# Attention and two gated layers on one core: a pair's softmax sums inverted as a row and spread over the partitions by way of DRAM

## Chip, core and metric

The kernel runs on one core of one Trainium2 chip. The metric is the device time of one execution in microseconds (us), as the median of several executions. Engines are named as in the profile: PE (matmul), PEld (PE's weight load, which overlaps the matmuls), DVE (vector engine), ACT (scalar engine), POOL (GpSimd), SP (the engine that issues all DMAs here).

## The reference, cut to what matters

Two batches, 8 heads, 1152 keys, head size 64; queries are averaged in pairs, so there are 576 queries per head. The output of attention is the input of a layer with a rational gate (512 to 2048 to 512), and that of a second layer with a SiLU gate (512 to 1536 to 512). The change is in attention's last line but one:

```python
q_pool = q.reshape(B, H, S // 2, 2, D).mean(axis=3)          # 576 queries
scores = scale * np.matmul(q_pool, k.transpose(0, 1, 3, 2))
scores = scores - np.max(scores, axis=-1, keepdims=True)
attn = np.exp(scores)
attn = attn / (np.sum(attn, axis=-1, keepdims=True) + 1e-09)
return np.matmul(attn, v).astype(np.float32)
```

The kernel multiplies the unnormalized exponentials with the values and divides by the sums afterwards.

## The kernel before, in words

**Stages.** Attention fills the first 290 us; the first layer follows, then a norm and the second layer. All matmuls are float32; the layers' weights come as 64-bit numbers and are converted in the kernel (lines 171 to 232), in part while attention runs. The converted pairs of that part are stored to DRAM (line 237, "spill") and fetched later.

**Attention.** The 16 heads are worked on in 8 pairs. A pair has 9 tiles of 128 queries (`TILES`): four of head 0, one shared by both heads (64 queries each), four of head 1. For a tile, PE makes the scores (L755), DVE takes their maximum (L784), ACT the exponentials and their sum into one column of `sums` [128 x 9] (L790), PE transposes the exponentials (L805), and DVE or ACT copy them out of PSUM into `pt` (L837, L840). The next tiles' scores go into the PSUM banks that these copies free.

**After the tiles of a head** (`pair_ops`, L867): 18 steps per head multiply the values with `pt` (L908; head size on the partitions, 576 queries in two halves of 288 columns, on partitions 0 to 63 and 64 to 127 of the one `av` bank). Two copies per head take the halves out of PSUM into `xt` [128 x 576], where head 0 has partitions 0 to 63 and head 1 the others (lines 589 and 592, which serve other copies too). The inverse sums have a query on each partition, while `xt` has a query in each column; so once per pair `f_rinv` adds 1e-9 and inverts [128 x 9] on DVE (L882, L883), `f_rx` spreads each inverse over 64 columns on POOL (L891, L893), `f_rows` transposes four blocks of 128 x 128 into the `prep` bank (L955) and `f_rT` a fifth into the `av` bank (L941), which ACT copies to `rxh` (L945). DVE then multiplies `xt`'s first 512 columns by the bank (`f_div`, L959), and POOL or DVE the last 64 by `rxh`, in two parts (`f_div_rest`, L964). Lines 592 and 605 split `xt` into the high and low parts `x_hi`, `x_lo` that the first layer reads. The bank `prep` has one buffer and serves the transposes of keys and queries as well (L703).

**What sets the order.** Operations are written down as `Op(engine, cost, key, function, needs, buffers)`, and `order()` places them in a planned time: on each engine the one of lowest key among those that can start now. An `op_any` may go to one of several engines. PE's tile and value steps are chained by a list written out by hand (`seq` in `attention`): scores of two tiles, up to five value steps, the transposes of both tiles. Each engine runs its operations in the planned order; a DMA counts 2000 ns in the plan from its issue to whoever needs it. All of attention and the first parts of the first layer (`FINE`) are placed in a first plan, the rest in a second, behind it on each engine.

Of the kernel before, what the change touches and what calls it, by code (L numbers as in the profile page):

```python
# [8 lines left out]
F32 = mybir.dt.float32  # L9
F32R = mybir.dt.float32r  # L10
U32 = mybir.dt.uint32
AF = mybir.ActivationFunctionType
ALU = mybir.AluOpType
AX = mybir.AxisListType
PSUM = bass.MemoryType.PSUM
# [4 lines left out]
def attention_moe_moe2_kernel(  # L20
# [18 lines left out]
    nc = tc.nc  # L39
    B, H, S, D = q.shape  # L40
    SQ = S // 2
# [8 lines left out]
    HALF = SQ % 128  # L50
    NFULL = SQ // 128
# [7 lines left out]
    def pool(tag, bufs=1, space=None):  # L59
        if tag not in pools:  # L60
            kw = {} if space is None else {"space": space}
            pools[tag] = scope[-1].enter_context(tc.tile_pool(name=tag, bufs=bufs, **kw))
# [3 lines left out]
    def T(tag, shape, dtype=F32, space=None):  # L66
        pool(tag, BUFS.get(tag, 1), space)
        return pools[tag].tile(shape, dtype, tag=tag, name=tag)
# [7 lines left out]
    ident = T("ident", [128, 128])  # L76
# [340 lines left out]
    PE, DVE, ACT, POOL = "PE", "DVE", "ACT", "POOL"  # L417

    def cost(eng, n):
        return {PE: 0.425 * n, DVE: 70 + 1.04 * n, ACT: 60 + 0.834 * n, POOL: 148 + 2.104 * n}[eng]  # L420
# [132 lines left out]
    NQ = NFULL + 1  # L553
# [4 lines left out]
    for h in range(2):  # L558
# [3 lines left out]
    NP = len(heads) // 2  # L562
    ABUF = {
        "kn": 2, "vn": 3, "qn0": 1, "qn1": 1, "qp": 2, "kT0": 1, "kT1": 1, "qT0": 1, "qT1": 1,
        "prep": 1, "av": 1, "p": 2, "pt": 3, "nm": 3, "sums": 2, "xt": 2, "rinv": 1, "rx": 1, "rxh": 1,
        "spill": 2,
    }
    BUFS.update(ABUF)
# [10 lines left out]
    NT = len(TILES)  # L579

    QW = SQ // 2
    TS = 3100

    def copy_ways(dst, src, n, psum=False, scale=None, fast=False, seen=lambda ins: None):

        by = 1.0 if scale is None else scale

        def on_act():
            seen(nc.scalar.activation(dst(), src(), AF.Copy, scale=by))

        def on(eng):
            seen(eng.tensor_scalar(dst(), src(), by, 1.0, op0=ALU.mult, op1=ALU.mult))

        ways = [(ACT, cost(ACT, n), on_act), (DVE, 70 + (0.52 if fast else 1.04) * n, lambda: on(nc.vector))]
        if not psum:
            ways.append((POOL, 30 + 1.08 * n, lambda: on(nc.gpsimd)))
        return ways

    def op_any(ways, key, deps=(), bufs=()):
        eng, c, fn = ways[0]  # L600
        return Op(eng, c, key, fn, deps, bufs, ways[1:])

    def sub_ways(out, a, b, n):
        def on(eng):
            eng.tensor_sub(out(), a(), b().bitcast(F32))

        return [(POOL, cost(POOL, n), lambda: on(nc.gpsimd)), (DVE, cost(DVE, n), lambda: on(nc.vector))]
# [125 lines left out]
    pt, pt_buf, pt_op, sums, sum_buf, sum_op, xt_ops, xt_buf, x_op = ({} for _ in range(9))  # L733
# [130 lines left out]
    LAST = [NFULL, 2 * NFULL]  # L864
    AVG = [[kt] for kt in range(NKT)]

    def pair_ops(pr):  # L867

        e = {}
        xb = Buf("xt")  # L870
        rb, rxb, rhb = Buf("rinv"), Buf("rx"), Buf("rxh")
        base = NT * pr * TS
        added = []

        def x_():
            if "x" not in e:
                e["x"] = T("xt", [128, SQ])
            return e["x"]

        def f_rinv():  # L880
            e["rinv"] = T("rinv", [128, NT])
            nc.vector.tensor_scalar_add(e["rinv"], sums[pr], 1e-9)  # L882
            nc.vector.reciprocal(e["rinv"], e["rinv"])  # L883

        def f_rx():
            rx = e["rx"] = T("rx", [128, NFULL + 1, 2, 64])
            rinv = e["rinv"]
            for h in range(2):
                r0 = h * (NFULL + 1)
                src = rinv[:, r0:r0 + NFULL].unsqueeze(2).to_broadcast([128, NFULL, 64])  # L890
                nc.gpsimd.tensor_scalar(rx[:, 0:NFULL, h, :], src, 1.0, 1.0, op0=ALU.mult, op1=ALU.mult)  # L891
            src = rinv[:, NFULL:NFULL + 1].unsqueeze(2).to_broadcast([128, 2, 64])
            nc.gpsimd.tensor_scalar(rx[:, NFULL], src, 1.0, 1.0, op0=ALU.mult, op1=ALU.mult)  # L893

        kr = base + NT * TS + 0
        o_rinv = Op(DVE, 330, kr, f_rinv, sum_op[pr], [sum_buf[pr], rb])
        o_rx = Op(POOL, 1050, kr + 300, f_rx, [o_rinv], [rb, rxb])

        for h in range(2):
            ab = Buf("av")  # L900
            last = None
            key = base + LAST[h] * TS + 9500

            def f_av(kt, h=h):
                if kt == 0:
                    e["av", h] = T("av", [128, 512], F32, space=PSUM)
                for c in range(2):
                    nc.tensor.matmul(  # L908
                        e["av", h][64 * c:64 * c + 64, 0:QW],
                        lhsT=v_tile[2 * pr + h][:, KEYS[kt], :],  # L910
                        rhs=pt[pr, h][:, kt, c * QW:(c + 1) * QW],
                        start=(kt == 0),
                        stop=(kt == NKT - 1),
                    )

            def f_avs(g, f=f_av):
                for kt in AVG[g]:
                    f(kt)

            for g in range(len(AVG)):  # L920
                last = Op(
                    PE, len(AVG[g]) * 0.84 * 2 * QW, key + 1350 * g, lambda g=g, f=f_avs: f(g),
                    [last, v_op[2 * pr + h], *pt_op[pr, h]], [ab, v_buf[2 * pr + h], pt_buf[pr, h]],
                )
                last.mode = "columns"
                av_ops.append((LAST[h] + NT * pr, last))
            key += 4000
            m = slice(64 * h, 64 * h + 64)
            for c in range(2):

                def src_(c=c, h=h):
                    return e["av", h][64 * c:64 * c + 64, 0:QW]

                def to_(c=c, m=m):
                    return x_()[m, c * QW:(c + 1) * QW]

                added.append(op_any(copy_ways(to_, src_, QW, True), key + 100 * c, [last], [ab, xb]))
            if h == 1:

                def f_rT():  # L940
                    nc.tensor.transpose(e["av", 1][:, 384:512], e["rx"][:, NFULL].rearrange("p a d -> p (a d)"), ident)  # L941

                def f_rxh():
                    e["rxh"] = T("rxh", [128, 128])
                    nc.scalar.activation(e["rxh"], e["av", 1][:, 384:512], AF.Copy)  # L945

                o_rT = Op(PE, 120, key - 200, f_rT, [o_rx, last], [ab, rxb])
                o_rxh = Op(ACT, 170, key - 100, f_rxh, [o_rT], [ab, rhb])

        pb = Buf("prep")  # L950

        def f_rows():
            e["rb"] = T("prep", [128, 512], F32, space=PSUM)
            for t in range(NFULL):
                nc.tensor.transpose(e["rb"][:, t * 128:t * 128 + 128], e["rx"][:, t].rearrange("p a d -> p (a d)"), ident)  # L955

        def f_div():
            x = e["x"]
            nc.vector.tensor_mul(x[:, 0:512], x[:, 0:512], e["rb"])  # L959

        def f_div_rest(eng):
            x = e["x"]
            for s in (slice(0, 64), slice(64, 128)):
                eng.tensor_mul(x[s, 512:SQ], x[s, 512:SQ], e["rxh"][s, s])  # L964

        o_rows = Op(PE, 460, key - 200, f_rows, [o_rx], [pb, rxb])
        o_div = [
            Op(DVE, 600, key + 800, f_div, [*added, o_rows], [pb, xb]),
            op_any(
                [(POOL, 566, lambda: f_div_rest(nc.gpsimd)), (DVE, 280, lambda: f_div_rest(nc.vector))],  # L970
                key + 800, [*added, o_rxh], [xb, rhb],
            ),
        ]
        b, hp = divmod(pr, H // 2)

        def xs(l):
            return (x_hi, x_lo)[l][:, hp, b * SQ:(b + 1) * SQ]

        o_xh = op_any(copy_ways(lambda: xs(0), x_, SQ, fast=True), key + 2000, o_div, [xb])
        x_op[b, hp] = op_any(sub_ways(lambda: xs(1), x_, lambda: xs(0), SQ), key + 2500, [o_xh], [xb])  # L980

    def f_warm():
# [513 lines left out]
```

## Time and profile before

| what | value |
|---|---|
| median of 3 executions | 745.83 us (742.72 to 746.51) |
| the profiled execution | 745.6 us |
| its span, first to last instruction | 743.8 us |
| PE, DVE, ACT, POOL busy, share of the span | 94%, 75%, 54%, 38% |
| mean granted clock of PE, share of the full 2.4 GHz | 0.986 |

The profile is of one execution. A busy share is an average over stages with different limits, and PE's matmuls are pipelined, so that two of them overlap in the records: the time from start to start of neighbours is what a matmul takes of the stream. The chain of waits follows the end back to what released each step; its shares say which engine's time went straight into the span.

### The profile page before, as it was taken

Reading aid. Unit: us, or ns where it says so; the run is one execution under the profiler, and the core shown is the slowest. Engines: PE = TensorE matmul, PEld = TensorE weight load, DVE = VectorE, ACT = ScalarE, POOL = GpSimd, SP = SyncE. Lnnn points to the kernel's source line nnn. Section 1 sums busy time; section 2 is a strip of 40 time slices with the busy share of each in tenths; the row PEclk is TensorE's granted clock in tenths of the full one; section 3 lists DMA queues with packets and bytes.
Section 4 is the critical chain, followed back from the end, with each engine's and each line's share of the span. In section 5 each row is a group of like instructions: output and inputs, shape, how many; then the busy total and the mean of one; then the engine's idle time right before and its main releaser. Section 6 shows DMA issues by size and latency. Waiting matters only on the chain.

```text
span 743.8 us, 13108 instructions
## 1 busy us (share of the span) xinstructions
PE 699.0 (94%) x5257; PEld 604.0 (81%) x5257; DVE 556.3 (75%) x723; ACT 403.4 (54%) x633; POOL 280.6 (38%) x245
## 2 busy tenths in 40 slices
PE   8899989998998999899999899899999999999997
PEld 7666666666666668889889799798999899989996
DVE  4799998988878773987977859957769346854844
ACT  4767677677777764898745756416423222312210
POOL 3032455645455520444442352326436123612500
PEclk9999989999999999999999999999999999999999
DMA  7444465446445330223104104000224202420103
GB/s 207 117 155 129 122 214 179 161 162 234 162 150 184 129 115 28 87 85 114 58 16 155 56 1 142 29 28 1 62 82 142 85 29 85 135 93 29 57 1 127
DMA packets 51596, 77.13 MB, mean 104 GB/s; under 512 B 4176, under 2 KB 33872, under 8 KB 51536
## 3 DMA queue, kind: packets, MB, share of 16 engines
q1 hardware_dynamic: 51536, 76.30, 31.6%
q8 instruction: 41, 0.67, 0.4%
q14 instruction: 19, 0.16, 0.1%
HBM read 61.87 MB, written 14.42 MB: 103 GB/s over the span
## 4 chain that ended last, share of the span: by engine, by line
PE 62%; DVE 20%; ACT 9%; issue 6%; POOL 2%; DMA 1%; SPq 0%; DVEq 0%; POOLq 0%; ACTq 0%
PE hid L498 22%; PE accp L498 16%; PE hid L755 9%; PE av L908 8%; PE hid L805 4%; DVE nm L784 2%; DVE pt L840 2%; ACT p L790 2%; DVE m_p L1132 2%; DVE m_q L1111 1%; DVE wc L186 1%; PE prep L703 1%; DVE m_q L1126 1%; ACT m_p L1098 1%; DVE wc L180 1%
## 5 line engine op out<-in xcount | busy, mean ns | idle before, releaser
L498 PE MATMUL hid<-x_hi,win_hi 128*128 128x384 f32 x480 | 162.3, 338 | 5.8 <-issue 2.8
L498 PE MATMUL hid<-x_lo,win_hi 128*128 128x384 f32 x480 | 161.5, 336 | 0.0
L498 PE MATMUL hid<-x_hi,win_lo 128*128 128x384 f32 x480 | 161.2, 336 | 0.0
L790 ACT ACTIVATE p<-hid,nm 128x1152 f32<-128x1152 f32 x72 | 87.7, 1220 | 31.0 <-DVE nm L784 30.5
L755 PE MATMUL hid<-kT,qT 64*128 64x256 f32 (+3 forms) x800 | 99.9, 383 | 3.8 <-DVE pt L840 3.3
L784 DVE TENSOR_REDUCE nm<-hid 128x1 f32<-128x1152 f32 x72 | 94.6, 1351 | 9.6 <-PE hid L755 8.6
L498 PEld LDWEIGHTS hid<-x_hi,win_hi 128*128 128x128 f32 x480 | 90.6, 189 | 8.7 <-issue 5.6
L498 PEld LDWEIGHTS hid<-x_lo,win_hi 128*128 128x128 f32 x480 | 90.6, 189 | 1.2 <-DVE x_lo L1304 0.3
L498 PEld LDWEIGHTS hid<-x_hi,win_lo 128*128 128x128 f32 x480 | 90.7, 189 | 0.0
L755 PEld LDWEIGHTS hid<-kT,qT 64*128 64x128 f32 (+1 forms) x800 | 75.4, 185 | 14.1 <-DVE pt L840 4.7
L805 PEld LDWEIGHTS hid<-ident,p 64*128 64x128 f32 x1296 | 54.3, 143 | 37.4 <-ACT p L790 17.2
L805 PE MATMUL hid<-ident,p 64*128 64x64 f32 x1296 | 69.2, 234 | 12.5 <-ACT p L790 10.1
L1146 POOL TENSOR_TENSOR g_lo<-m_p,g_hi 128x1152 fp32r<-128x1152 f32 (+1 forms) x20 | 47.0, 2360 | 88.0 <-ACT g_hi L1143 88.0
L498 PE MATMUL accp<-g_hi,wout_hi 128*128 128x384 f32 x192 | 66.1, 344 | 11.3 <-DVE acc L1201 9.9
L908 PE MATMUL av<-pt,vn 128*64 128x288 f32 x576 | 76.7, 411 | 0.0
L837 ACT ACTIVATE pt<-hid 128x512 f32<-128x512 f32 (+2 forms) x130 | 55.7, 461 | 31.1 <-PE hid L805 28.4
L199 POOL TENSOR_SCALAR win_hi<-wc 128x512 fp32r<-128x512 f32 x25 | 16.2, 648 | 135.8 <-PE hid L498 105.6
L840 DVE COPY pt<-hid 128x512 f32<-128x512 f32 (+2 forms) x94 | 51.7, 567 | 18.4 <-PE hid L805 18.1
L498 PE MATMUL accp<-g_lo,wout_hi 128*128 128x384 f32 x192 | 64.9, 338 | 0.2 <-POOL g_lo L1146 0.2
L498 PE MATMUL accp<-g_hi,wout_lo 128*128 128x384 f32 x192 | 64.8, 337 | 0.0
L171 ACT ACTIVATE wc<-wraw 128x512 f32<-128x512 f32 x68 | 45.9, 674 | 34.7 <-POOL wout_lo L204 15.8
L908 PEld LDWEIGHTS av<-pt,vn 128*64 128x64 f32 x576 | 38.6, 136 | 26.5 <-issue 1.9
(121 smaller groups left out, 1274.0 us busy)
## 6 DMA issues: line engine op xcount, KB each, us to landing
wraw<-in_moe_w_out_dram SPq DMA_DIRECT2D x28, 512.0 KB, 3.5
far<-spill SPq DMA_DIRECT2D x23, 512.0 KB, 3.5
wraw<-in_moe_w_in_dram SPq DMA_DIRECT2D x16, 512.0 KB, 3.8
wraw<-in_moe_w_gate_dram SPq DMA_DIRECT2D x12, 512.0 KB, 3.5
wraw<-in_moe_w_val_dram SPq DMA_DIRECT2D x12, 512.0 KB, 3.9
kn<-in_k_dram SPq DMA_DIRECT2D x16, 288.0 KB, 3.9
vn<-in_v_dram SPq DMA_DIRECT2D x16, 288.0 KB, 3.8
qn<-in_q_dram SPq DMA_DIRECT2D x16, 256.0 KB, 3.1
```

Source lines behind the costliest of these rows:

```text
L171: nc.scalar.activation(c.bitcast(F32), wt["raw", n][:, :, 1].bitcast(F32), AF.Abs, scale=2.0**-112)
L199: eng.tensor_scalar(hi, w_float(n), 1.0, 1.0, op0=ALU.mult, op1=ALU.mult)
L498: ins = nc.tensor.matmul(dst, lhsT=a[x], rhs=b[y], start=first and i == 0 and p == 0, stop=last and i == n - 1 and p == 2,)
L755: ins = nc.tensor.matmul(ps[to, j, c:c + x1 - x0], lhsT=qT[2 * pr + h][rows, c0:c0 + to.stop - to.start], rhs=kT[2 * pr + h][rows, x0:x1], ...
L784: nc.vector.tensor_reduce(out=e["nm"], in_=scores(), op=ALU.max, axis=AX.X, negate=True)
L790: nc.scalar.activation(e["p"], scores(), AF.Exp, bias=e["nm"], scale=1.0, accum_out=sums[pr][:, t:t + 1])
L805: ins = nc.tensor.transpose(ps[:, g, c:c + 64], e["p"][rows, 128 * j:128 * j + 128], ident[rows, rows])
L837: return nc.scalar.activation(to, src, AF.Copy)
L840: return nc.vector.tensor_copy(to, src)
L908: nc.tensor.matmul(e["av", h][64 * c:64 * c + 64, 0:QW], lhsT=v_tile[2 * pr + h][:, KEYS[kt], :], rhs=pt[pr, h][:, kt, c * QW:(c + 1) * QW ...
L1132: stt(p_(), p_(), na0, u_(), op0=ALU.add, op1=ALU.mult)
L1146: eng.tensor_sub(g_(1), p_(), g_(0).bitcast(F32))
```

## The change

`f_rinv`, `f_rx`, `f_rows`, `f_rT`, `f_rxh`, `f_div` and `f_div_rest` go. For each head, `over_sums` transposes its five columns of sums on PE ([128 x 5] to [5 x 128] in the `prep` bank), adds 1e-9 and inverts there on DVE, stores the five rows to DRAM, and reads them back as one line per half, the same for 64 partitions each, into `over` [128 x 288]: two reads for head 0, three for head 1, whose first 64 queries stand in the shared tile. The copies out of `av` become multiplications by `over`, on DVE alone.

```diff
-        "prep": 1, "av": 1, "p": 2, "pt": 3, "nm": 3, "sums": 2, "xt": 2, "rinv": 1, "rx": 1, "rxh": 1,
+        "prep": 1, "av": 1, "p": 2, "pt": 3, "nm": 3, "sums": 2, "xt": 2, "rows": 2, "over": 2,
...
-        def f_rinv():
-            e["rinv"] = T("rinv", [128, NT])
-            nc.vector.tensor_scalar_add(e["rinv"], sums[pr], 1e-9)
-            nc.vector.reciprocal(e["rinv"], e["rinv"])
-
-        def f_rx():
...
-        kr = base + NT * TS + 0
-        o_rinv = Op(DVE, 330, kr, f_rinv, sum_op[pr], [sum_buf[pr], rb])
-        o_rx = Op(POOL, 1050, kr + 300, f_rx, [o_rinv], [rb, rxb])
+        R0 = [0, NFULL]
+        rows_of = [
+            [(0, 0, 0, QW), (1, 0, QW, 2 * QW)],
+            [(0, 0, 128, 128 + QW), (1, 0, 128 + QW, 128 + 128 * NFULL), (1, 128 * NFULL - QW, HALF, 128)],
+        ]
+        over_op, over_buf = {}, {}
+
+        def over_sums(h):
+            pb, rb, ob = Buf("prep"), Buf("rows"), Buf("over")
+            over_buf[h] = ob
+            i = 2 * pr + h
+
+            def f_T():
+                e["rT", h] = T("prep", [128, 512], F32, space=PSUM)
+                nc.tensor.transpose(e["rT", h][0:NQ, 0:128], sums[pr][:, R0[h]:R0[h] + NQ], ident)
+
+            def f_over():
+                r = e["rows", h] = T("rows", [NQ, 128])
+                nc.vector.tensor_scalar_add(r, e["rT", h][0:NQ, 0:128], 1e-9)
+                nc.vector.reciprocal(r, r)
+
+            def f_far():
+                d = e["far", h] = T(f"over{i}", [NQ, 128], space=bass.MemoryType.DRAM)
+                nc.sync.dma_start(out=d, in_=e["rows", h])
+
+            def f_near():
+                o = e["over", h] = T("over", [128, QW])
+                d = e["far", h].rearrange("t p -> (t p)")
+                for c, at, x0, x1 in rows_of[h]:
+                    nc.sync.dma_start(out=o[64 * c:64 * c + 64, at:at + x1 - x0], in_=d[x0:x1].partition_broadcast(64))
+
+            k = base + LAST[h] * TS + 2600
+            o_T = Op(PE, 120, k, f_T, sum_op[pr][R0[h]:R0[h] + NQ], [sum_buf[pr], pb])
+            o_o = Op(DVE, 420, k, f_over, [o_T], [pb, rb])
+            o_f = Op("SP", 400, k, f_far, [o_o], [rb])
+            over_op[h] = Op("SP", 800, k, f_near, [o_f], [ob])
...
-                added.append(op_any(copy_ways(to_, src_, QW, True), key + 100 * c, [last], [ab, xb]))
-            if h == 1:
...
-                o_rT = Op(PE, 120, key - 200, f_rT, [o_rx, last], [ab, rxb])
-                o_rxh = Op(ACT, 170, key - 100, f_rxh, [o_rT], [ab, rhb])
...
-        o_rows = Op(PE, 460, key - 200, f_rows, [o_rx], [pb, rxb])
-        o_div = [
-            Op(DVE, 600, key + 800, f_div, [*added, o_rows], [pb, xb]),
...
+                def f_div(c=c, h=h, m=m):
+                    part = slice(64 * c, 64 * c + 64)
+                    nc.vector.tensor_mul(x_()[m, c * QW:(c + 1) * QW], e["av", h][part, 0:QW], e["over", h][part])
+
+                added.append(Op(DVE, cost(DVE, QW), key + 100 * c, f_div, [last, over_op[h]], [ab, xb, over_buf[h]]))
...
-        o_xh = op_any(copy_ways(lambda: xs(0), x_, SQ, fast=True), key + 2000, o_div, [xb])
+        o_xh = op_any(copy_ways(lambda: xs(0), x_, SQ, fast=True), key + 2000, added, [xb])
```

## Rows read from the trace of the kernel before

**Rows 1.** Windows: length, PE, PEld, DVE, ACT, POOL busy us (x instructions), clock, DMA share, GB/s.

```profile
32.00:292.00 260.00, 243.79 (x2686) 174.01 (x2686) 219.21 (x322) 182.77 (x351) 118.81 (x126) 0.99 0.47 153
50.00:100.00 50.00, 46.32 (x517) 33.40 (x513) 48.55 (x74) 35.06 (x70) 22.17 (x23) 0.95 0.42 128
270.00:280.00 10.00, 9.22 (x118) 6.78 (x115) 6.78 (x11) 7.13 (x15) 0.73 (x2) 1.00 0.01 3
```

**Rows 2.** The chain of waits, 32 to 292 us: shares of its time by line.

```profile
by line: PE av L908 22.1%; PE hid L755 21.4%; PE hid L805 9.7%; issue 7.3%; DVE pt L840 6.6%; DVE nm L784 5.2%; ACT p L790 3.9%; PE prep L703 3.6%; DVE xt L592 2.5%; PE hid L498 2.1%; DVE wc L176 1.4%; DVE wc L186 1.3%; DVE xt L959 1.1%; DV
```

**Rows 3.** PE in time order: start us, length us; pair 3 (of 8), then one piece of the chain.

```profile
124.00 2.16 PE L908 MATMUL av<-pt,vn 128*64 128x288 f32 x16
126.09 0.33 PE L941 MATMUL av<-ident,rx 128*128 128x128 f32 x1
126.35 0.77 PE L805 MATMUL hid<-ident,p 64*128 64x64 f32 x17
...
50.20 0.59 PE prep L955 x4
```

**Rows 4.** DVE groups by shape, 30 to 290 us: busy us, mean ns | idle before.

```profile
L592 DVE TENSOR_SCALAR xt<-av 64x288 f32<-64x288 f32 x26 | 11.8, 455 | 5.5 <-PE av L908 3.0 <-PE av L941 2.2
L959 DVE TENSOR_TENSOR xt<-xt,prep 128x512 f32<-128x512 f32 x7 | 4.8, 680 | 0.1
L964 DVE TENSOR_TENSOR xt<-xt,rxh 64x64 f32<-64x64 f32 x6 | 2.0, 326 | 0.0
L883 DVE RECIPROCAL rinv<-rinv 128x9 f32<-128x9 f32 x8 | 1.7, 216 | 0.3
L592 DVE TENSOR_SCALAR kT<-prep 64x128 f32<-64x128 f32 x6 | 1.6, 275 | 0.1
```

**Rows 5.** One line, L882: ns min/median/max, first and last start.

```profile
L882 DVE TENSOR_SCALAR rinv<-sums x8: 159/164/706, 41.5 to 278.7; 128x9 f32<-128x9 f32 x8
```

**Rows 6.** DVE in time order, after the value steps of a head 1.

```profile
128.14 0.69 DVE L959 TENSOR_TENSOR xt<-xt,prep 128x512 f32<-128x512 f32 x1
128.74 1.10 DVE L964 TENSOR_TENSOR xt<-xt,rxh 64x64 f32<-64x64 f32 x2
129.88 0.46 DVE L592 TENSOR_SCALAR x_hi<-xt 128x576 fp32r<-128x576 f32 x1
130.26 0.88 DVE L840 COPY pt<-hid 128x512 f32<-128x512 f32 x2
```

**Rows 7.** Waits of DVE, 32 to 292 us: us in total, times, longest.

```profile
DVE pt L840 <- PE hid L805: 14.9, 25, 1.8
```

**Rows 8.** DMA issues: count, KB each, median us to landing.

```profile
out_dram<-acc SPq DMA_DIRECT2D x9, 256.0 KB, 2.0
coef<-in_moe_b_dram SPq DMA_DIRECT2D x1, 1.0 KB, 4.0
wout_lo<-far SPq DMA_DIRECT2D x10, 256.0 KB, 5.0
```

**Rows 9.** Waits of SP's queue, whole span: us in total, times, longest.

```profile
SPq L162 <- DVE wc L186: 259.0, 42, 42.0
```

**Rows 10.** Time order at the end of attention.

```profile
276.61 1.23 ACT L790 ACTIVATE p<-hid,nm 128x1152 f32<-128x1152 f32 x1
278.71 0.16 DVE L882 TENSOR_SCALAR rinv<-sums 128x9 f32<-128x9 f32 x1
...
290.43 0.28 ACT L945 ACTIVATE rxh<-av 128x128 f32<-128x128 f32 x1 [4.50 <-PE av L941]
290.74 0.82 ACT L589 ACTIVATE xt<-av 64x288 f32<-64x288 f32 x2
...
292.88 0.76 DVE L605 TENSOR_TENSOR x_lo<-xt,x_hi 128x576 fp32r<-128x576 f32 x1
...
299.67 0.51 PE L498 MATMUL hid<-x_hi,win_hi 128*128 128x384 f32 x1 [1.98 <-DVE m_p L1104]
```

**Rows 11.** A window after attention, columns as in rows 1.

```profile
310.00:320.00 10.00, 8.52 (x46) 7.88 (x47) 9.97 (x16) 9.04 (x13) 3.12 (x3) 1.00 0.36 110
```

More of the change, by code (lines that the diff above doesn't have):

```diff
@@ L870, in pair_ops @@
         xb = Buf("xt")
-        rb, rxb, rhb = Buf("rinv"), Buf("rx"), Buf("rxh")
         base = NT * pr * TS
@@ L878, in x_ @@
             return e["x"]
-        def f_rinv():
-            e["rinv"] = T("rinv", [128, NT])
-            nc.vector.tensor_scalar_add(e["rinv"], sums[pr], 1e-9)
-            nc.vector.reciprocal(e["rinv"], e["rinv"])
-        def f_rx():
[L886 to L893, printed above, removed]
@@ L899, in pair_ops @@
+        over_sums(0)
+        over_sums(1)
         for h in range(2):
@@ L929, in pair_ops @@
             for c in range(2):
[L931 to L935, printed above, removed]
-                added.append(op_any(copy_ways(to_, src_, QW, True), key + 100 * c, [last], [ab, xb]))
-            if h == 1:
[L940 to L945, printed above, removed]
-                o_rT = Op(PE, 120, key - 200, f_rT, [o_rx, last], [ab, rxb])
-                o_rxh = Op(ACT, 170, key - 100, f_rxh, [o_rT], [ab, rhb])
[L950 to L964, printed above, removed]
-        o_rows = Op(PE, 460, key - 200, f_rows, [o_rx], [pb, rxb])
-        o_div = [
-            Op(DVE, 600, key + 800, f_div, [*added, o_rows], [pb, xb]),
[L969 to L973, printed above, removed]
+                def f_div(c=c, h=h, m=m):
+                    part = slice(64 * c, 64 * c + 64)
+                    nc.vector.tensor_mul(x_()[m, c * QW:(c + 1) * QW], e["av", h][part, 0:QW], e["over", h][part])
+                added.append(Op(DVE, cost(DVE, QW), key + 100 * c, f_div, [last, over_op[h]], [ab, xb, over_buf[h]]))
         b, hp = divmod(pr, H // 2)
```

## Prediction

> **What bounds the kernel now.** I read the windows first, for attention is where the change lies. In its 260 us PE is busy 243.8, DVE 219.2, ACT 182.8 [rows 1]: PE leads, but DVE is close, and between 50 and 100 us DVE is the fuller of the two (48.55 of 50). So I went to the chain of waits of the same stretch [rows 2]: PE's lines shown there make 58.9% of it (22.1 + 21.4 + 9.7 + 3.6 + 2.1), DVE's 18.1%, ACT's 3.9%, "issue" 7.3%; the remaining 11.8% are small lines that the row cuts off, which I put with DVE. Attention is thus a loop in which PE, DVE and ACT take turns: of a microsecond taken off PE some 0.6 should come out of the span, and one put on DVE should add some 0.3. Third came the order on DVE [rows 6]: after the values of a head 1, `f_div` and its rest run ahead of the copies into `pt` that free PSUM for the next scores. Last I read the end of attention [rows 10], where nothing covers the division.
>
> **PE.** Each pair loses `f_rows`, 0.59 us of the stream, and `f_rT`, whose start is 0.26 us ahead of its follower's (126.09 to 126.35) [rows 3]: 0.85, and 6.8 us over 8 pairs. It gains two transposes per pair. None of that shape is in the trace; four in a row took 0.59, or 0.15 each, and one alone 0.26, so I take 0.2: 16 x 0.2 = 3.2. Net -3.6 (-2.6 to -4.4), and at 0.6 of it **-2.1 us**.
>
> **DVE.** Removed, over 8 pairs [rows 4, 5]: 26 copies out of `av` 11.8 us, `f_div` 8 x 0.68 = 5.4, the DVE share of its rest 2.0, the add 8 x 0.164 = 1.3, the reciprocal 1.7; together 22.2. Added: 32 multiplications of 64 x 288, all on DVE. The copy of that shape took 0.455 and the multiplication of 512 columns 0.68; the cost goes with columns, so I take the former: 14.6. Then 16 times `f_over`. Its add reads 128 columns from PSUM, as the 64 x 128 copy did in 0.275. Its reciprocal is the open price. On nine columns it took 216 ns, 52 more than the add's median 164 of that shape [rows 4, 5]. If the 52 belong to the instruction, 128 columns take 0.275 + 0.05 = 0.33 us; if they belong to the columns (5.8 ns each), 0.275 + 0.74 = 1.02. I take 1.02, since the copies and multiplications of rows 4 differ by their columns and not by their kind. So `f_over` costs 1.29 us (low end 0.61), where the plan counts 0.42; that is 20.6 us, and DVE's net is +13.0 (low end +2.1). At 0.3, **+3.9 us**.
>
> The Trainium skill, "VectorE: DVE Perf Modes", section "Walkthrough: the 8-slice pipeline in each mode", has the reciprocal as an iterative divide with a repeat count of 8; at the 0.96 GHz of its specifications I estimate 1.07 us for 128 columns alone, and DVE's net would be some 3 us higher with the fixed part on top. The two rows of nine columns lean that way, but no row here has a long reciprocal. Were the page wrong, the low end holds and the term would be 0.6 us in place of 3.9.
>
> **ACT and POOL.** ACT loses 8 copies into `rxh` of 0.28 and six copies of 0.41 (one of the first and two of the second stand in [rows 10]): 4.7 us; at its 3.9% **-0.2**. POOL loses the spreading and part of the rest; none of its lines is among those of the chain shown, so nothing. That cover is DVE's and PE's work; were it gone, the loss would still be a gain.
>
> **SP and the way by DRAM.** Seven DMAs per pair, 56 in all, are issued on SP. The store waits for DVE, and the reads wait for the store to land. Behind them in SP's queue stand loads of keys, queries and values, weight loads and the spill stores. SP waits 259 us in one line alone for buffers to come free [rows 9], and by 270 us the transfers are over (DMA share 0.01, [rows 1]), 20 us before the stage ends; so I cost this at nothing. Without that cover, each of 16 waits of 2.0 to 5.0 us [rows 8] would push weight conversion later. Whether the line of inverses is there in time: the last head's sums are complete at about 278.0 (276.61 + 1.23 and the read of the sum), and its values are done just before 290.1 (ACT waits for the transpose behind them until 290.43) [rows 10], so there are 12 us. The way takes 0.3 to the transpose's end, 1.3 for `f_over`, and two landings of 2.0 to 5.0 [rows 8]: 5.6 to 11.6. It fits, so I cost it at nothing.
>
> **Keys' and queries' bank.** `prep` is held from `f_rows` to `f_div` before, and only across `f_over` afterwards, twice per pair. PE's transposes of keys and queries may gain or lose by it; no row gives a price. An end for that, and for the order being planned anew, is the 16.2 us in which PE is not busy in 260 [rows 1]. I take zero.
>
> **The handover.** After the last values, ACT makes `rxh` and two copies, DVE `f_div`, `x_hi` and `x_lo`, until 293.64: 3.5 us from 290.1 [rows 10]. Afterwards two multiplications (0.91), the copy into `x_hi` (0.46, [rows 6]) and `x_lo` (0.76) need 2.1. DVE comes 1.4 us earlier to the first layer, and ACT is out of this step. DVE fills the stretch that follows (9.97 of 10, [rows 11]), and PE waits 1.98 us for it at 299.67. Between nothing (another wait takes its place) and 2.0 I take **-1.2**.
>
> **Sum**: -2.1 + 3.9 - 0.2 - 1.2 = +0.4. The profiled execution took 745.6 (span 743.8 and 1.8 around it), 0.2 under the median of the runs; 746.0 against 745.83 is no change.
>
> **The rivals.**
>
> *Slower: `f_over` ahead of the copies into `pt`.* By its key it comes before the copies of the head's last tile, at the moment when PE needs them for the next scores, and all 16 are like that. DVE waits for these transposes 14.9 us in 25 times, 0.6 each [rows 7]; the rest of 1.29, 0.7, goes into the loop: 16 x 0.7 = +11.0. Against it stand PE's -2.1, `f_div`'s place on the chain (1.1% of 260 us, [rows 2]) -2.9, and -1.2 at the handover: +4.8, or 751. For it speaks that the plan counts 0.42; against it, that ACT can take some of the copies. It decides from about 0.6 us lost per `f_over` ((3.7 + 6.2)/16).
>
> *Slower by the DMAs.* With both landings at 5.0 and one such transfer ahead of them, the last pair comes 4.6 us late, and DVE stands still in front of the multiplication: 751. Only the last rows of the DMA list speak for it.
>
> *Faster: DVE's waits swallow `f_over`.* DVE is idle 40.8 of 260 us [rows 1], 2.5 us per `f_over`, or the reciprocal has its low price. Then PE's 3.6 come out whole, `f_div`'s 2.9 leave the chain, the handover gives 2.0: -8.5, or 737. For it speaks that `f_div` and its rest, 1.7 us ahead of a `pt` copy [rows 6], do go; against it, that DVE has little idle time from 50 to 100 us.
>
> **How the numbers follow.** A measurement of this kernel can tell about 0.5%, 3.7 us, from no change. I give no change 0.38 (its own range 742 to 749.5), the faster case 0.31, the slower ones 0.31, of which 0.04 to the DMAs. The range of 8 in 10 goes from 739 to 753: it holds the slower price and most of the way to the faster one; beyond it lie the whole of -8.5 and the whole of DVE's 13 us.
>
> **What would show it.** Right: a reciprocal of about 1.0 us on 5 x 128 and `f_over` of 1.3; multiplications of 0.45; DVE in attention some 13 us busier and PE less; in the waits, PE's waits for `pt` copies up; no wait of DVE for a DMA; first-layer work on DVE some 1.4 us sooner after the last values. Wrong: a reciprocal of 0.33 us, or DVE's waits before `pt` copies gone with PE's waits unchanged (faster), or DVE waiting for `over`, or PE waiting a whole `f_over` 16 times (slower).

## The result, and the profile after

The changed kernel took 754.12 us (median of 5 executions, 750.77 to 754.86) against 745.83 of the kernel before: ratio 1.0101, 95% interval [1.0073, 1.0129]. It is 8 us slower, where no change was forecast, and lies 1 us above the range. Run once more beside other kernels it gave 754.5, ratio 1.0116 [1.0088, 1.0145].

The page of the kernel after, its head and its row of granted clocks (40 slices of 18.8 us), and the windows with the columns of [rows 1]:

```profile
span 753.0 us, 13113 instructions
...
PE 702.6 (93%) x5233; PEld 604.6 (80%) x5233; DVE 565.1 (75%) x730; ACT 397.5 (53%) x613; POOL 273.9 (36%) x218
...
PEclk9699979999999999999999999999999999999999
```

```profile
32.00:292.00 260.00, 238.01 (x2619) 169.11 (x2618) 227.97 (x328) 177.39 (x332) 114.34 (x99) 0.97 0.49 159
50.00:100.00 50.00, 44.78 (x492) 30.96 (x491) 48.49 (x67) 31.93 (x62) 19.25 (x19) 0.97 0.45 137
```

Against [rows 1] DVE has 8.8 us more work in the 260 us, ACT 5.4 and POOL 4.5 less, and PE got 5.8 us less done: it waited. The granted clock of the stretch fell from 0.99 to 0.97. In the slices marked `6` and `7` the clock stood for a time at the lower of its two levels, 1.2 GHz. The first such stretch lies at 19 to 32 us. Between 10 and 20 us PE was busy for 6.6 us; the second trace of the same kernel has 6.5 there, and no fall behind it.

The chain of waits of the same stretch, to be read against [rows 2]:

```profile
by line: PE hid L755 19.1%; PE av L930 13.2%; issue 9.8%; DVE nm L784 9.2%; PE hid L805 7.6%; DVE pt L840 6.8%; ACT p L790 4.4%; DVE wc L176 4.2%; PE prep L703 3.8%; DVE xt L955 2.7%; DVE rows L900 2.3%; DMA kn<-in_k_dram 2.2%; DVE kT L592 
```

The product with the values has fallen from 22.1% to 13.2% of the chain, the maximum on DVE has risen from 5.2% to 9.2%, and the new reciprocal (L900) is on it with 2.3%, 6.0 us: the loop has moved some way from PE towards DVE (the lines shown make 43.7% for PE and 25.2% for DVE, 58.9% and 18.1% before). The DVE groups by shape (30 to 300 us) give the prices, which answer to [rows 4, 5]:

```profile
L955 DVE TENSOR_TENSOR xt<-av,over 64x288 f32<-64x288 f32 x32 | 14.5, 454 | 14.8 <-PE av L930 13.6 <-issue 0.6
L900 DVE RECIPROCAL rows<-rows 5x128 f32<-5x128 f32 x15 | 14.1, 941 | 0.5
...
L899 DVE TENSOR_SCALAR rows<-prep 5x128 f32<-5x128 f32 x15 | 4.1, 272 | 1.2 <-PE prep L895 1.2
```

Add and reciprocal take 1.21 us per head. In the order of time they look like this, PE with its weight loads and DVE only, at the end of a head 0:

```profile
173.80 0.78 PE L805 MATMUL hid<-ident,p 64*128 64x64 f32 x18 [0.28 <-ACT p L790]
173.97 0.27 DVE L899 TENSOR_SCALAR rows<-prep 5x128 f32<-5x128 f32 x1
...
174.27 0.94 DVE L900 RECIPROCAL rows<-rows 5x128 f32<-5x128 f32 x1
...
174.41 1.09 PE L755 MATMUL hid<-kT,qT 64*128 64x256 f32 x8
...
175.14 0.87 DVE L840 COPY pt<-hid 128x64 f32<-128x64 f32 x3
...
175.42 0.20 PEld L703 LDWEIGHTS prep<-ident,qp 128*128 128x128 f32 x2 [0.33 <-DVE pt L840]
...
175.79 0.27 PE L805 MATMUL hid<-ident,p 64*128 64x64 f32 x1
...
175.91 1.52 PE L755 MATMUL hid<-kT,qT 64*128 64x128 f32 x12
...
176.38 2.62 DVE L784 TENSOR_REDUCE nm<-hid 128x1 f32<-128x1152 f32 x2
```

The copies into `pt` stand behind the reciprocal, PE waits for them (0.33 us at 175.42), its next scores start at 175.91, and the next maximum only at 176.38. The wait of PE's weight loads for these copies, 28 to 290 us (us in total, times, longest), first of the kernel before, then of the changed one, and the wait of SP's queue:

```profile
PEld hid L755 <- DVE pt L840: 4.7, 9, 1.3
```

```profile
PEld hid L755 <- DVE pt L840: 11.0, 14, 1.3
```

```profile
SPq L904 <- DVE rows L900: 75.9, 13, 12.3
```

SP stood 76 us, in 13 times, in front of the 16 stores. What the profile does not have is a wait of DVE for the read lines: in the DVE groups above, L955 waited for PE's values and 0.6 us for nothing shown.

**Where the 8 us arose.** The start of the last exponentials (tile 71) is a mark for the end of attention, the first unit's `g_hi` (a unit is one block of 128 rows of the first layer's hidden size) one for the first layer. For the changed kernel:

```profile
285.95 1.22 ACT L790 ACTIVATE p<-hid,nm 128x1152 f32<-128x1152 f32 x1
```

| | last exponentials start | from there to the first `g_hi` | span |
|---|---|---|---|
| before | 276.61 | 28.72 | 743.8 |
| after | 285.95 | 27.06 | 753.0 |

In these two executions attention lost 9.3 us. (The profiled execution of the changed kernel, 754.86 us, is the longest of its five.) At the handover 1.7 us came back, by the `g_hi` of the fifth unit 1.5 more; but from the tenth unit to the fourteenth the first layer took 56.1 us where it had taken 53.3, and most of it was given back.

### The profile page after: what moved, and what is told of

It is laid out like the page before. It is cut to its first block, busy times and chain, and to the rows that moved or that the text cites. A ratio compares the mean times of both kernels' runs of the same rounds, so it can differ in the third digit from the quotient of the medians.

```text
span 753.0 us, 13113 instructions
## 1 busy us (share of the span) xinstructions
PE 702.6 (93%) x5233; PEld 604.6 (80%) x5233; DVE 565.1 (75%) x730; ACT 397.5 (53%) x613; POOL 273.9 (36%) x218
## 4 chain that ended last, share of the span: by engine, by line
PE 53%; DVE 23%; ACT 10%; issue 7%; DMA 3%; POOL 2%; SPq 0%; POOLq 0%; DVEq 0%; ACTq 0%
PE hid L498 21%; PE accp L498 14%; PE hid L755 8%; PE av L930 5%; DVE nm L784 4%; PE hid L805 3%; ACT p L790 2%; DVE pt L840 2%; DVE m_q L1096 2%; DVE wc L176 2%; DVE m_p L1117 1%; DMA kn<-in_k_dram 1%; PE prep L703 1%; DVE wc L186 1%; DVE acc L1186 1%
## 5 line engine op out<-in xcount | busy, mean ns | idle before, releaser
L755 PE MATMUL hid<-kT,qT 64*128 64x256 f32 (+3 forms) x800 | 102.7, 391 | 8.4 <-DVE pt L840 8.1
L755 PEld LDWEIGHTS hid<-kT,qT 64*128 64x128 f32 (+1 forms) x800 | 77.9, 187 | 21.6 <-DVE pt L840 11.0
```

Of the source, the lines that this page charges most:

```text
L755: ins = nc.tensor.matmul(ps[to, j, c:c + x1 - x0], lhsT=qT[2 * pr + h][rows, c0:c0 + to.stop - to.start], rhs=kT[2 * pr + h][rows, x0:x1], ...
```

## The experiments

Theory A: the reciprocal on DVE lengthens attention's loop. Theory B: SP's queue, standing in front of the stores, brings loads late. Theory C: the order, planned anew, is a worse one whatever an instruction takes. Ratios are to the kernel before on the same chip.

**e1, no reciprocal, order unchanged.**

```diff
-                nc.vector.reciprocal(r, r)
```

> The changed kernel with the 16 reciprocals of 5x128 left out (the sums themselves are stored, so the products are multiplied where they should be divided); the plan, and so the order on every engine, is that of the changed kernel. Theory A (the reciprocal, 0.94 us on DVE against 0.22 before, in front of the copies that PE waits for, makes attention longer): 744 to 748 us, 6 to 10 below the changed kernel's 754. Theory B (SP's queue stands in front of the stores, up to 12.3 us, and the loads behind them come late): 751 to 754, as the stores still wait for the same place on DVE. Theory C (the order as planned anew is the worse one, whatever an instruction takes): 752 to 755.

Measured: 745.99 us, 1.0004 [0.9976, 1.0032]. All of the loss is gone; in the profile the last exponentials start at 275.70. In this order 15.0 us of reciprocal on DVE cost about 8 us (1.0101 or 1.0116 less 1.0004, 7 to 8 us), 0.5 of its time. A holds; what is left of the change comes out at no change.

Part of this cost comes with PE's granted clock, third from the end in the windows of the first 300 us (the kernel before, the changed kernel, e1):

```profile
0.00:300.00 300.00, 276.13 (x2964) 201.36 (x2965) 243.95 (x365) 207.15 (x400) 124.54 (x137) 0.98 0.47 153
```

```profile
0.00:300.00 300.00, 272.56 (x2901) 195.19 (x2902) 245.48 (x358) 194.28 (x366) 120.05 (x110) 0.95 0.49 158
```

```profile
0.00:300.00 300.00, 273.08 (x2955) 198.70 (x2956) 245.60 (x361) 203.50 (x384) 120.37 (x111) 0.99 0.50 162
```

What the clock is worth can be read from executions of one kernel: those of the kernel before, run beside e1, that had a mean granted clock of 0.993 took 743.2 to 743.9 us, those that had 0.984 took 746.5 to 747.8, some 0.4 us per 0.001. The changed kernel's eleven executions average 0.982 and e1's twelve 0.987. By this estimate about 2 of the 7 to 8 us go with the clock, and 5 to 6 are left at the same clock. What made the clock fall more often no run shows.

**e2, the inverse before the transpose.**

```diff
+            def f_inv():
+                v = e["inv", h] = T("inv", [128, NQ])
+                nc.vector.tensor_scalar_add(v, sums[pr][:, R0[h]:R0[h] + NQ], 1e-9)
+                nc.vector.reciprocal(v, v)
...
-                nc.vector.tensor_scalar_add(r, e["rT", h][0:NQ, 0:128], 1e-9)
-                nc.vector.reciprocal(r, r)
+                nc.vector.tensor_scalar(r, e["rT", h][0:NQ, 0:128], 1.0, 1.0, op0=ALU.mult, op1=ALU.mult)
```

> The changed kernel with the inverse taken on the 128 x 5 columns before the transpose, and a copy out of PSUM after it: 0.16 + 0.19 + 0.27 = 0.62 us of DVE per head in place of 0.27 + 0.94 = 1.21, and one more wait between engines. Theory A: 0.59 x 16 = 9.4 us off DVE, of which some 4 to 6 come out: 748 to 750. Theory B: 752 to 755. Theory C: planned anew again, so anywhere from 748 to 757, without a tie to DVE's waits.

Measured: 755.9, 1.0143 [1.0117, 1.0170], with the last exponentials at 288.88. Less DVE time, and slower: a miss for A by itself. In the trace DVE's part is 0.90 us per head, not the 0.62 expected (add 0.44, reciprocal 0.19, copy 0.27: the add took 0.17 at the median, but up to 0.93), against 1.21. Something else costs as much as was saved. Some of it goes with the clock: e2's executions average 0.979, which by e1's estimate is some 3 us against a kernel at 0.987. PE's transposes waited only 1.8 us for the inverse.

**e3, no way by DRAM, order unchanged.** The body of `f_far` goes, and `f_near` gives a constant tile in place of the lines read.

```diff
-                nc.sync.dma_start(out=d, in_=e["rows", h])
...
-                for c, at, x0, x1 in rows_of[h]:
-                    nc.sync.dma_start(out=o[64 * c:64 * c + 64, at:at + x1 - x0], in_=d[x0:x1].partition_broadcast(64))
+                e["over", h] = fixed
```

> The changed kernel without its 16 stores and 40 reads (the products are multiplied by a constant line instead of the inverses, which are still computed); the plan keeps their places, so all other instructions stand in the order of the changed kernel. Theory A: 753 to 755, no gain. Theory B: SP's 76 us of waiting in front of the stores go, and loads of keys, queries and weights are issued earlier: 745 to 749. Theory C: 752 to 755.

Measured: 752.86, 1.0091 [1.0061, 1.0122]. The 56 DMAs and SP's 76 us cost 1 us or nothing. B falls: what stood behind the stores in SP's queue can hardly have been needed sooner.

**e4, the plan told the true cost.**

```diff
-            o_o = Op(DVE, 420, k, f_over, [o_T], [pb, rb])
+            o_o = Op(DVE, 1250, k, f_over, [o_T], [pb, rb])
```

> The changed kernel with the planned cost of the add and reciprocal at 1250 ns, what they take, in place of 420: the same instructions, another order. Theory A: DVE has as much to do; the plan can only place it better: 749 to 754. Theory B: stores are planned later, so SP waits less in front of them (under 30 us in place of 76): 746 to 750. Theory C: 748 to 758, either way.

Measured: 751.6, 1.0086 [1.0055, 1.0118]: not told apart from the changed kernel. A right price did not make the plan a good one.

**The changed kernel again**, beside the next three.

> The changed kernel itself, beside the others on the same chip: 752 to 756 us by every theory.

Measured: 754.5, 1.0116 [1.0088, 1.0145].

**e5, the inverse on ACT** (`b_sum` holds 1e-9).

```diff
-                nc.vector.tensor_scalar_add(r, e["rT", h][0:NQ, 0:128], 1e-9)
-                nc.vector.reciprocal(r, r)
+                nc.scalar.activation(r, e["rT", h][0:NQ, 0:128], AF.Ln, bias=b_sum[0:NQ], scale=1.0)
+                nc.scalar.activation(r, r, AF.Exp, scale=-1.0)
...
-            o_o = Op(DVE, 420, k, f_over, [o_T], [pb, rb])
+            o_o = Op(ACT, 420, k, f_over, [o_T], [pb, rb])
```

> The inverse made on ACT, as exp(-ln(sum + 1e-9)) in two instructions of 5 x 128 straight from PSUM, planned as an ACT operation of 420 ns; DVE loses add and reciprocal, 1.21 us per head. Theory A (DVE's reciprocal, 0.94 us, costs the loop about half of itself): the 8 us of the reciprocals come back and the add's part too: 742 to 747. Theory C (the planned order is what decides): 748 to 757, as this is another order with as many instructions. A rival, that ACT is as tight as DVE: 747 to 751.

Measured: 743.78, 0.9991 [0.9965, 1.0018]: as A expected, the change without DVE's reciprocal is no slower than the kernel before.

**e6, three reciprocals in a row, order unchanged.**

```diff
-                nc.vector.reciprocal(r, r)
+                nc.vector.reciprocal(r, r); nc.vector.reciprocal(r, r); nc.vector.reciprocal(r, r)
```

> The changed kernel with the reciprocal taken three times in a row, which gives the same inverse, in the unchanged order: 16 x 2 x 0.94 = 30 us more of DVE. Theory A, each at the 0.5 that one of them cost: 768 to 772; more than that (up to 780) if DVE has no waits left that take part of it. If the first reciprocals' 8 us were a threshold (the clock that falls, a wait that tips over) and not DVE's time: under 762.

Measured: 800.47, 1.0728 [1.0683, 1.0772]. Thirty microseconds more on DVE cost 46, more than any theory had. The window of 32 to 292 us, with the granted clock third from the end:

```profile
32.00:292.00 260.00, 220.32 (x2178) 153.44 (x2177) 222.01 (x313) 153.49 (x285) 112.31 (x98) 0.88 0.46 156
```

The price is not a fixed share. The first 0.94 us per head is half hidden by waits of DVE; the next two are not, and PE, which waits more, also runs at a lower granted clock (0.88 of 2.4 GHz against 0.97). Over whole executions the mean is 0.955 against 0.982; by e1's estimate, carried far outside the values it was read from, some 11 of the 46 us go with the clock.

**e7, the same instructions with a later key.**

```diff
-            k = base + LAST[h] * TS + 2600
+            k = base + LAST[h] * TS + 5600
```

> The changed kernel with the key of the new operations 3000 ns later (5600 in place of 2600), so that add and reciprocal stand behind the copies into pt of the head's last tile and the next maximum; every instruction is the same. If it is the place ahead of those copies that makes the reciprocal dear: 746 to 750. If it is DVE's load, wherever it stands: 752 to 756, with the waits of PE moved to another line. Theory C: either way by some us.

Measured: 746.37, 1.0007 [0.9987, 1.0028]. With nothing taken away, the loss is gone. In the DVE order of the changed kernel 13 of the 16 reciprocals stand directly in front of a copy into `pt` or a maximum; here 4 do, and most of the others are followed by weight conversion, for which nobody waits. PE's wait for the copies is back near the 4.7 us of the kernel before:

```profile
PEld hid L755 <- DVE pt L840: 5.1, 10, 1.2
```

This is what the place would give, and also what a luckier order would. The next three bear on which it is.

**e8, e7 without its reciprocals, in e7's order** (the edit of e1).

> The kernel with the later key (e7) with its 16 reciprocals left out, in e7's order (the sums are stored, so the products are multiplied where they should be divided). If the place ahead of the copies into pt and of the maxima made the reciprocal dear, it costs next to nothing behind them: 743 to 746, as e7. If e7 is only a luckier order and the reciprocal costs its 8 us there too: 736 to 740.

Measured: 742.82, 0.9956 [0.9940, 0.9973]; last exponentials at 271.99. So in e7's order the reciprocals cost 0.0051, some 4 us: half of what they cost in the changed kernel, and not nothing. Between the two expectations.

**e10, another order with the reciprocals in the same kind of place.**

```diff
-            o_o = Op(DVE, 420, k, f_over, [o_T], [pb, rb])
+            o_o = Op(DVE, 800, k, f_over, [o_T], [pb, rb])
```

> The changed kernel with its key, and 800 ns as the planned cost of add and reciprocal in place of 420: another order on DVE, in which 13 of the 16 reciprocals still stand directly in front of a copy into pt or a maximum (15 of 16 with 1250 ns, 13 in the changed kernel, 4 with the later key). Theory of the place: 751 to 756. Theory C (every new order gives its own time): as likely 744 to 750.

Measured: 747.26, 1.0018 [1.0003, 1.0034]. A miss for the theory of the place: the neighbours of the reciprocals are of the same kind, and 7 us are gone, at the same mean clock (0.983, the changed kernel 0.982).

**e12, e10 without its reciprocals, in e10's order** (the edit of e1).

> e10 (planned cost 800) with its 16 reciprocals left out, in e10's order (the sums are stored, so the products are multiplied where they should be divided). If the reciprocal costs its 8 us in any order that has it ahead of the copies and maxima: 738 to 741, and e10's order is 7 us better by itself than the changed kernel's. If it costs what it does behind them (3 to 4 us in e7's order): 743 to 745.

Measured: 744.17, 0.9996 [0.9982, 1.0011]. Here they cost 0.0022, about 2 us (from nothing to 3). The mean clocks of the pairs differ too: 0.987 and 0.985 with and without reciprocals in e7's order, 0.983 and 0.989 in e10's. By e1's estimate the three prices at the same clock are 5 to 6, 4 to 5 and about nothing: the clock does not bring them together.

**e11, e2 with the later key**, and **e9, e5 with the later key** (the edit of e7).

> The inverse on the columns before the transpose (as e2, which came out at 756 although DVE had 9.4 us less to do) with the later key. Theory of the place: its add, reciprocal and copy stand behind the copies into pt too, 743 to 748. If e2's loss has another cause (the way DVE, PE, DVE, on which PE waits for the inverse): 750 to 757.

Measured: 753.88, 1.0088 [1.0066, 1.0110]. The later key, which gave e7 8 us, gave this one 0.0055, some 4 us; its interval just clears that of e2. The rest of its loss is not explained by the place, nor by PE's waiting for the inverse, which is 2.9 us in the trace; it stays open.

> The inverse on ACT (as e5) with the later key (as e7). Theory of the place: on ACT it took nothing measurable off e1's time, so there is little left to gain: 741 to 745. If ACT's two instructions in front of its copies cost what DVE's did: 739 to 741.

Measured: 746.28, 0.9992 [0.9971, 1.0014]: no better than e5, and above both expectations.

**e13 and e14, the kernel before with only its order planned anew.** The operations are the same; in the traces the order of DVE's some 720 instructions differs in 151 and 54 lines, a few of which went to another engine (`op_any`).

```diff
-        o_rinv = Op(DVE, 330, kr, f_rinv, sum_op[pr], [sum_buf[pr], rb])
+        o_rinv = Op(DVE, 500, kr, f_rinv, sum_op[pr], [sum_buf[pr], rb])
```

> The kernel before with only the planned cost of its inversion changed, 500 ns in place of 330: the same instructions, planned anew. If the planned order is worth several us either way (theory C): off 746 by over 3 us, sooner up than down if the kernel before had a good draw. If it is worth little: 744 to 748.

```diff
-        o_rows = Op(PE, 460, key - 200, f_rows, [o_rx], [pb, rxb])
+        o_rows = Op(PE, 600, key - 200, f_rows, [o_rx], [pb, rxb])
```

> The kernel before with only the planned cost of f_rows changed, 600 ns in place of 460: fewer places of the order change than in e13. Theory C: off 746 by over 2 us; otherwise 744 to 748.

Measured: 749.15, 1.0064 [1.0041, 1.0086], and 747.53, 1.0054 [1.0031, 1.0076]. The kernel before loses 4 to 5 us by its ratios when nothing is changed but two planned costs, one at a time, and hardly by the clock (0.988 and 0.987 against 0.989 of the kernel before beside them). The order it came with is better than these two, and a change that makes the plan anew gives it up.

**e15, the version that should beat both**: e7's order on every engine, the inverse issued on ACT (e5's two instructions at the place of DVE's, the plan still counting 420 ns of DVE).

> The kernel with the later key (e7), in e7's order on every engine, with the inverse issued on ACT as exp(-ln(sum + 1e-9)) at the place where DVE had add and reciprocal. e8, e7's order without the reciprocal, took 742.8; DVE loses the add too, ACT gains two short instructions: 741 to 744, faster than the kernel before by about 0.4%. If ACT's part costs as much as DVE's reciprocal did there: 746.

Measured: 741.31, 0.9954 [0.9929, 0.9979], 0.46% faster than the kernel before. Its two ACT groups, 0.65 us per head in place of DVE's 1.21:

```profile
L901 ACT ACTIVATE rows<-prep,b_sum 5x128 f32<-5x128 f32 x16 | 5.5, 346 | 0.5 <-PE prep L897 0.5
...
L902 ACT ACTIVATE rows<-rows 5x128 f32<-5x128 f32 x16 | 4.9, 308 | 0.5
```

## Why the prediction was wrong, point by point

**What bounds the kernel**: right as far as it went. Attention is a loop of PE, DVE and ACT, and the change moved weight to DVE. But the 11.8% of small lines were not all DVE's: summed by engine, the chain before is 60.6% PE, 23.8% DVE, 6.6% ACT. With 0.24 in place of 0.3 DVE's term would have been +3.1, further off.

**PE, -2.1.** The two transposes per pair take 0.20 us of the chain where they are on it, as taken. That the removed five gave 2.1 us no run shows by itself.

**DVE, the prices**: right. The multiplication is 0.454 us (0.455 taken), the add 0.272 (0.275), the reciprocal 0.941 (1.02), so `f_over` takes 1.21 (1.29): the 52 ns belong to the columns, and the time rises by (941 - 216)/119 = 6.1 ns per column. DVE's balance was +8.8 us over the span (556.3 to 565.1), not +13.0; these prices give +11.7, and the rest lies in other work of the new plan, which I did not follow. The Trainium skill, "VectorE: DVE Perf Modes", section "Walkthrough: the 8-slice pipeline in each mode", has the reciprocal as an iterative divide with a repeat count of 8; my estimate from it, 1.07 us for 128 columns alone, is above the measured 0.941.

**DVE, +3.9**: the step that failed first. "One put on DVE should add some 0.3" is a share of the chain before, an average over 260 us; `f_over` is not spread over them. Of its +3.9, 0.3 x 1.02 x 16 = 4.9 were the reciprocals' and -1.0 the rest of DVE's balance. Measured in the changed kernel's order, the reciprocals cost 7 to 8 (e1), about 2 of it with the granted clock, for which the prediction had no term.

**The price taken from an average for one place** was the wrong tool both ways: the same reciprocals cost 8, 4 and 2 us in three orders (e1, e8, e12), and 1.5 us per us when two more were added to each (e6).

**The rest, -4.5** (0.4 less 4.9): the step that failed second. Measured without the reciprocal in the same order it is +0.3 us, within 2 either way (e1). I wrote of the order being planned anew, "I take zero". e13 and e14 show what that is worth for the kernel before: +4.8 and +4.0. The three orders of the change without a reciprocal (e1, e8, e12) stand at 1.0004, 0.9956 and 0.9996, on average 0.74% or 5.5 us under the two replanned kernels before (1.0059 on average). So the savings may have been about as large as I worked out, and a lost order may have eaten them. This last step is an inference from five orders, not shown by any run.

**ACT and POOL, -0.2; the keys' and queries' bank, nothing**: ACT lost 5.4 us in the window and POOL 4.5, and PE's transposes into `prep` hold 3.8% of the chain after 3.6%. What either is worth no run shows by itself.

**The handover, -1.2**: right. From the last values to the end of `x_lo` it took 2.3 us in place of 3.5, and the first `g_hi` came 1.7 us sooner. It was given back between the tenth unit and the fourteenth. Of the 2.8 us there, 1.2 stand in every trace of the changed kernel, e1's too (19.0 us in place of 17.8 from the tenth unit to the eleventh); what costs them I have not tried. The other 1.6 go with a fall of the clock to 1.2 GHz at 435 us (0.83 over 430 to 440): e1 and e12, which have no such fall there, take 16.5 us from the thirteenth unit to the fourteenth, like the kernel before, and the traces with one take 17.9, e13 among them.

**SP and DRAM, nothing**: right (e3), though SP waited 76 us in front of the stores. DVE never waited for the lines read.

**The rivals.** The slower one had the mechanism, `f_over` ahead of the copies that PE waits for (11.0 us in place of 4.7), at 751. Its price was 3 us short: its loss of 11.0 was above what the reciprocals cost, but it set the savings of 6.2 against it in full, and e1 shows that in this order nothing of them was left. Its rule for when it decides (place) is not the whole of it, since e10 has the same kind of place and 747. What in an order makes a reciprocal cost 8 or 2 us stays open. The faster rival, that DVE's waits swallow `f_over`, is nearly true of the reciprocals in e10's order (2 of 15 us), but that kernel takes 747 and not 737.

## What to carry to other kernels

Where a program plans the order of a tuned kernel, run the kernel before once or twice with one harmless planned cost changed: here that alone was worth 0.5 to 0.6%, as much as most edits, and a change should be judged against that spread. The reciprocal went by its columns, however few partitions it had; turning the sums into a line first multiplied its time (0.22 us on 9 columns per pair, 2 x 0.94 on 128). Set the mean granted clocks of the executions beside their times before explaining a difference of 1%: here 0.005 of it went with some 2 us. When an instruction's price may depend on its place, take it out and put it back in the same order before blaming the queue, and move it by its key before moving it to another engine.

## What the runs showed that was not expected

Adding 30 us to DVE in an unchanged order cost 46 us of the span (e6): PE waited more, and the granted clock of attention was 0.88 in place of 0.97. And SP's queue stood 76 us in all in front of stores that waited for DVE, with no effect that could be told from none (e3: 1.0091 against 1.0101).
